# Attention and maxout MLP in one kernel: opening two products of the first layer when the first head group is done

## The chip, the cores and the metric

The kernel runs on one core of a Trainium2 chip. The metric is the device time of one execution in microseconds (us). Engines are named as in the profile: PE (TensorE), DVE (VectorE), ACT (ScalarE), POOL (GpSimd), SP (the queue that issues DMAs).

## The reference

For 8 batches of 8 heads, 576 positions and head size 64, two attentions are added: one over queries, keys and values that are averaged in fours (its output is repeated four times), and one in which each position sees only the positions less than 4 away. The sum, seen as 4608 tokens of 512 features, goes through a maxout MLP with 768 hidden features.

```python
out_d = sm_attn(q_d, k_d, v_d)            # pooled by 4
out_up = np.repeat(out_d, factor, axis=2)
mask = np.abs(pos[:, None] - pos[None, :]) < factor
scores = np.where(mask, scale * q @ k.T, -1e9)
x = out_up + softmax(scores) @ v          # -> (4608, 512)
h = np.maximum(np.maximum(x @ w1, x @ w2), x @ w3)
return h @ w_out
```

## The kernel before, in words

Nothing is issued where it is written. The program first records operations with their tiles; `place` (line 287) then plays a list scheduler with prices for each operation and gives every engine a fixed order, and `emit` (line 414, whence line 458 in all rows) issues in that order. An operation is offered when its inputs are done and its buffers can be had; among those offered an engine takes the one with the smallest priority number (`at(prio, lag)`, line 484), PE operations with a priority of 0 or more ahead of those with a negative one (line 210). The constants at lines 36 to 45 and 81 to 89 are lags, margins, priorities and prices of that scheduler. Buffers of one tag, PSUM banks too, are given out strictly in the order in which the tiles were written in the program (lines 312 to 328): a later tile of the tag cannot take a buffer before an earlier one has. There are four banks `pm`, three `pa` and one `pq` (line 481).

A head group n is four heads of one batch; a block j is the two groups 2j and 2j + 1 of a batch's first 512 positions. The first two blocks are computed on PE by `dense(j)` (line 1130): band scores (`band_scores`, two pairs of heads `pr`, each in two steps `tp` of two banks, softmax on DVE and ACT with maxima `mxb` and sums `zb`), pooled inputs (`band_sums`), band values (`band_values`, which transposes the probabilities in two banks for each pair and multiplies in `pq`), and the pooled attention (`pooled`, line 1136, through `tail_pooled`, `pooled_scores`, `band_pooled_values`, `pooled_values`). Block 0 uses the `pm` banks, block 1 the `pa` banks. The other blocks compute the band on DVE, POOL and ACT (`scores`, `values`).

`turn(j)` (line 1166) adds pooled and band outputs for each of four feature columns c (two from each head group) and splits the sum into a high and a low part, `xhi` and `xlo` (`transposes`, line 888). `mlp_column(j, ft, tag)` (line 910) computes one of six groups of 128 hidden features: for each of the three weights i it opens one bank and sums 12 products into it, for each column c high x high, low weight x high, high weight x low; then it takes the maximum. `mlp_out` (line 927) does the second layer. Weights arrive as 64-bit floats and are cut up in pieces by `weight_split` (line 570) on ACT and DVE: `weight_in(ft)` makes the three pieces of one hidden group, `whi` and `wlo`. Pieces have a priority of 39.08 plus 0.91 for each piece (line 1173).

The order in which block 0 is written (line 1152) gives the order of the `pm` banks: scores of group 0, values of group 0, scores of group 1, values of group 1, and only then, from `mlp_column(0, 0, "pm")` (line 1190), the first layer. The priorities of the groups are `FIRST` (line 43); `LATE` (line 44) is added for the loads of the pooled inputs (`late`, line 606): 37.8 for group 1.

Of the kernel before, what the change touches and what calls it, by code (L numbers as in the profile page):

```python
# [21 lines left out]
P = 128  # L22
# [5 lines left out]
NCC = DM // P  # L28
# [4 lines left out]
QS = 1.0 / 128.0  # L33
QB = 1.0 / 8.0
XBUFS = 5
LAG = 646.33
LAG0 = 272.7
MLP = 601.0
PE_LAG = 1784.3
BANK_LAG = 1458.35  # L40
SEG = FAC * P
NDENSE = 2
FIRST = (0.0, 5.15, 43.52, 45.57)
LATE = (0.0, 37.8, 0.0, 0.0)
WPRIO = (20.0, 60.0, 105.0, 150.0, 160.0, 170.0, 180.0)
SETS = (5, 4, 3, 2, 5, 4, 5, 5)
HOMES = ("whi5", "whi4", "whi3", "whi2", "pv", "pv", "whi5", "pv")
# [30 lines left out]

ENGINES = ("PE", "DVE", "ACT", "POOL", "SP")
DONE_NS = {"PE": 230.0, "DVE": 150.0, "ACT": 190.0, "POOL": 200.0}  # L80
SPARE = 1850.93
PATIENCE = {"PE": 0.0, "DVE": 294.88, "ACT": 136.05, "POOL": 0.0, "SP": 0.0}
LANES = 8
RING = 128
DMA_FIRST = 1300.0
# [1 line left out]
SLOW = 82000.0  # L87
SWITCH = {("R", "P"): 120.0, ("P", "R"): 110.0, ("P", "T"): 25.0, ("T", "P"): 93.0, ("t", "P"): 90.0, ("P", "t"): 90.0, ("B", "P"): 96.0, ("M", "P"): 100.0, ("P", "M"): 20.0, ("R", "T"): 10.0, ("T", "R"): 5.0, ("R", "M"): 91.0, ("T", "M"): 93.0, ("M", "R"): 300.0, ("M", "T"): 305.0, ("M", "B"): 0.0, ("B", "M"): 96.0, ("B", "R"): 120.0, ("t", "R"): 90.0, ("R", "t"): 95.0, ("t", "M"): 90.0, ("t", "B"): 90.0, ("t", "T"): 90.0, ("T", "t"): 90.0, ("M", "t"): 100.0}
COLD = 1.65


def is_ap(a):
# [56 lines left out]
class Recorder:  # L149
# [44 lines left out]
    def add(self, forms):  # L194

        o = Op()
        o.forms = forms
        outs, ins = [], []
        for method, args, kw in next(iter(forms.values())):
            named = [k for k in ("out", "accum_out") if is_ap(kw.get(k))]  # L200
            w = [kw[k] for k in named]
            r = [a for a in args if is_ap(a)] + [v for k, v in kw.items() if is_ap(v) and k not in named]
            if "out" not in named:
                w.append(args[0])
                r = r[1:]
            outs += w
            ins += r
        o.prio = self.prio
        if "PE" in forms and o.prio >= 0.0:
            o.prio -= 2000.0  # L210
        o.lag, o.spare, o.margin = self.lag, self.spare, 0.0
        if "PE" in forms and self.lag in (LAG, MLP):
            o.lag, o.margin = PE_LAG, BANK_LAG
        elif self.lag == MLP:
            o.lag = 0.0
        o.seq = len(self.ops)
        o.need, o.tiles = set(), []
        pe = "PE" in forms
        for write, aps in ((False, ins), (True, outs)):
            for ap in aps:  # L220
                r = self.region(ap)
                if r is None:
                    continue
                info, p0, p1, m = r
                bufs, order = self.tags[info["tag"]]
                assert info["k"] + bufs >= len(order), ("used after its buffer was given on", info["name"])
                for q, w, a0, a1, am, was_pe in info["acc"]:
                    if (w or write) and q is not o and (info["psum"] or (a0 < p1 and p0 < a1 and (am & m))):
                        o.need.add(q)
                if not info["ops"] or info["ops"][-1] is not o:  # L230
                    info["ops"].append(o)
                    o.tiles.append(info)
                if write and info["psum"] and pe:
                    info["acc"] = [x for x in info["acc"] if not (x[1] and x[5])]
                info["acc"].append((o, write, p0, p1, m, pe))
        self.ops.append(o)
        return o
# [49 lines left out]
    def place(self):  # L287
# [45 lines left out]
        while len(out) < len(ops):  # L333
# [30 lines left out]
            if e == "PE":  # L364
                kind = pe_kind(o)
                c += SWITCH.get((last_kind, kind), 0.0)
                last_kind = kind
            if e == "PE" and t < SLOW:
                c *= COLD
            o.eng, o.start = e, t  # L370
            if e == "SP":
# [98 lines left out]
def local_global_attention_maxout_kernel(ctx: ExitStack, tc: tile.TileContext, q, k, v, qt_dense, kt_dense, qt_pool, kt_pool, qkt_tail, v_dense, v_tail, w_in, w_out, ident_d, mask_d, band_d, out):  # L470
# [89 lines left out]
    def load_constants():  # L560
        for t in ptail + dtail:
            dve.memset(t, 0.0)
        load_band()
        for t in vt2:
            dve.memset(t[0:3, 0], 0.0)

# [340 lines left out]
        blk["lo"].append(lo)  # L907


    def mlp_column(j, ft, tag):  # L910
        blk = state["blk", j]
        t = new([P, 4 * P], tag="t", bufs=3, name=f"t_{j}_{ft}")
        for i in range(3):
            ps = bank([P, 4 * P], tag, f"ph_{j}_{ft}_{i}")
            ops = [(a[ft][:, i, c], b[c]) for c in range(NCC) for a, b in ((whi, blk["hi"]), (wlo, blk["hi"]), (whi, blk["lo"]))]
            for m, (a, b) in enumerate(ops):
                pe.matmul(ps, a, b, start=m == 0, stop=m == len(ops) - 1)
            if i == 0:
                act.copy(t, ps)
            else:  # L920
                dve.tensor_tensor(out=t if i == 1 else ps, in0=ps, in1=t, op=ALU.max)
        h = new([P, 2, 4 * P], F32R, tag=f"whi{ft}" if j == B else f"hh{ft}", name=f"h_{j}_{ft}")
        blk["h"][ft] = h
        act.copy(h[:, 0], ps)
        dve.tensor_tensor(out=h[:, 1], in0=ps, in1=h[:, 0].bitcast(F32), op=ALU.subtract)
# [204 lines left out]
    def dense(j):  # L1130
        tag = "pm" if j == 0 else "pa"
        ns = (2 * j, 2 * j + 1)
        state["blk", j] = {"x": [None] * NCC, "band": {}, "hi": [], "lo": []}
        prio = {n: FIRST[n] for n in ns}

        def pooled(n, _):
            tail_pooled(n)
            pooled_scores(n)
            band_pooled_values(n)
            pooled_values(n)  # L1140

        def step(n, f, *a):
            with at(prio[n], LAG0):
                f(n, *a)

        a, b = ns
        load = {n: [(n, band_load), (n, band_load_v)] for n in ns}
        scores = {n: [(n, band_scores, pr, tag) for pr in range(2)] for n in ns}
        sums = {n: [(n, band_sums, pr, tag) for pr in range(2)] for n in ns}
        values = {n: [(n, band_values, pr, tag) for pr in range(2)] for n in ns}  # L1150
        if j == 0:
            order = [load[a][0], load[b][0], load[a][1], load[b][1]] + scores[a] + sums[a] + values[a] + scores[b] + sums[b] + values[b] + [(a, pooled, 0), (b, pooled, 0)]
        else:
            order = load[a] + scores[a] + sums[a] + values[a] + load[b]
            order += [scores[b][0], sums[b][0], (a, pooled, 0), values[b][0], scores[b][1], sums[b][1], values[b][1], (b, pooled, 0)]
        for x in order:
            step(*x)
# [5 lines left out]
                attention(n)  # L1163
        rec.spare = 0.0

    def turn(j):
        with at(-200.0, LAG0 if j < 2 else LAG):
            for c in range(NCC):
                transposes(j, c)

    def weights(f, *which):
        for x in which:
            with at(39.08 + state["pieces"] * 0.91):
                f(x)

    with at(-2.0):
        load_constants()
    dense(0)
    weights(weight_in, 0, 1, 2)
    turn(0)  # L1180
    weights(weight_in, 3)
    weights(weight_out, 0, 1, 2, 3)
    dense(1)
# [63 lines left out]
```

## Time and profile before

| | us |
|---|---|
| median of 3 runs | 742.31 (741.31 to 744.15) |
| profiled execution, its own time | 743.23 |
| span of the profiled execution | 741.5 |
| PE busy in the span | 716.1 (97%) |
| DVE busy | 643.0 (87%) |
| ACT busy | 438.8 (59%) |
| POOL busy | 364.2 (49%) |

The profiled execution is 0.92 us above the median; 1.73 us of its time lie around the span. Busy shares are means over stages with different limits, so the stage matters: the queries below cut the span. Every row carries line 458, since one helper issues everything, so rows are told apart by their tiles: `xhi_0r`, `xlo_0r`, `whi_0r`, `wlo_0r` are the split activations and weights of the first layer, `hqk` the weight piece being cut up, `whi`, `wlo` without `_0r` buffers that hold the band's inputs and probabilities early on, `nm` and `pa` belong to the pooled attention.

### The profile page before, as it was taken

Reading aid. Unit: us, or ns where it says so; the run is one execution under the profiler, and the core shown is the slowest. Engines: PE = TensorE matmul, PEld = TensorE weight load, DVE = VectorE, ACT = ScalarE, POOL = GpSimd, SP = SyncE. Lnnn points to the kernel's source line nnn. Section 1 sums busy time; section 2 is a strip of 40 time slices with the busy share of each in tenths; the row PEclk is TensorE's granted clock in tenths of the full one; section 3 lists DMA queues with packets and bytes.
Section 4 is the critical chain, followed back from the end, with each engine's and each line's share of the span. In section 5 each row is a group of like instructions: output and inputs, shape, how many; then the busy total and the mean of one; then the engine's idle time right before and its main releaser. Section 6 shows DMA issues by size and latency. Waiting matters only on the chain.

```text
span 741.5 us, 11907 instructions
## 1 busy us (share of the span) xinstructions
PE 716.1 (97%) x3820; PEld 569.4 (77%) x3820; DVE 643.0 (87%) x961; ACT 438.8 (59%) x1486; POOL 364.2 (49%) x563
## 2 busy tenths in 40 slices
PE   5977999999999999999999999999999999999996
PEld 3765677878787877778877887788778888888885
DVE  6999998999989996989989997979998999988520
ACT  4776867627595738657484849575785646433221
POOL 0100001139895977668387949495875735321000
PEclk9969899999999999999999999999999999999999
DMA  8943334365645362555346434532442310000012
GB/s 285 360 168 124 101 91 143 96 201 180 193 127 181 122 194 83 153 165 178 93 130 190 150 103 150 166 98 87 153 122 89 107 60 15 2 1 0 1 57 57
DMA packets 51561, 92.21 MB, mean 124 GB/s; under 512 B 5644, under 2 KB 21310, under 8 KB 51498
## 3 DMA queue, kind: packets, MB, share of 16 engines
q1 hardware_dynamic: 51498, 91.45, 39.2%
q8 instruction: 30, 0.49, 0.3%
q14 instruction: 33, 0.27, 0.1%
HBM read 81.99 MB, written 9.44 MB: 123 GB/s over the span
## 4 chain that ended last, share of the span: by engine, by line
PE 89%; DVE 4%; ACT 2%; DMA 2%; POOL 1%; issue 0%; SPq 0%; ACTq 0%; POOLq 0%; DVEq 0%
PE pm L458 73%; PE pa L458 14%; PE pq L458 2%; DVE hqk L458 1%; ACT wlo L458 1%; DVE x L458 1%; DMA hh<-in_w_in_dram 1%; DMA v<-in_v_dram 1%; DMA whi<-in_kt_dense_dram 1%; DVE wlo_0r L458 1%; DVE mxb L458 0%; POOL pv L458 0%; DVE xlo_0r L458 0%; DVE t L458 0%; SPq L458 0%
## 5 line engine op out<-in xcount | busy, mean ns | idle before, releaser
L458 PE MATMUL pm<-xhi_0r,whi_0r 128*128 128x512 f32 x552 | 219.2, 397 | 0.8 <-ACT xhi_0r L458 0.8
L458 PE MATMUL pm<-xhi_0r,wlo_0r 128*128 128x512 f32 x552 | 218.7, 396 | 0.0
L458 PE MATMUL pm<-xlo_0r,whi_0r 128*128 128x512 f32 x552 | 218.5, 397 | 0.0
L458 ACT ACTIVATE pv<-v,sums 128x64 f32<-128x64 f32 x604 | 158.1, 416 | 12.6 <-POOL sums L458 9.1
L458 POOL TENSOR_TENSOR pv<-v,sums 128x256 f32<-128x256 f32 x227 | 137.6, 708 | 5.9 <-DMA v<-in_v_dram 5.2
L458 PE MATMUL pm<-wo_0r,hh_0r 128*128 128x512 f32 x576 | 137.4, 393 | 0.0
L458 PEld LDWEIGHTS pm<-wo_0r,hh_0r 128*128 128x128 f32 x576 | 107.0, 188 | 23.4 <-issue 0.9
L458 PEld LDWEIGHTS pm<-xhi_0r,whi_0r 128*128 128x128 f32 x552 | 104.4, 189 | 23.5 <-issue 1.1
L458 PEld LDWEIGHTS pm<-xlo_0r,whi_0r 128*128 128x128 f32 x552 | 104.5, 189 | 22.3 <-issue 0.8
L458 PEld LDWEIGHTS pm<-xhi_0r,wlo_0r 128*128 128x128 f32 x552 | 104.6, 189 | 22.0 <-issue 0.9
L458 DVE TENSOR_REDUCE sums<-prod 128x28 f32<-128x1792 f32 x56 | 113.5, 2027 | 0.4
L458 DVE TENSOR_TENSOR prod<-k,pq 128x1792 f32<-128x1792 f32 x56 | 112.4, 2007 | 0.5
L458 DVE TENSOR_REDUCE x<-pv 128x256 f32<-128x1792 f32 x34 | 73.5, 2162 | 10.2 <-ACT pv L458 8.2
L458 POOL TENSOR_TENSOR pv<-pv 128x768 f32<-128x768 f32 (+1 forms) x44 | 68.3, 1552 | 6.0 <-ACT pv L458 4.2
L458 ACT CAST hh_0r<-pm 128x512 fp32r<-128x512 f32 x48 | 28.4, 591 | 48.8 <-DVE pm L458 48.6
L458 ACT COPY y<-pm 128x512 f32<-128x512 f32 x46 | 26.8, 589 | 48.9 <-PE pm L458 43.7
L458 POOL TENSOR_TENSOR hv<-v 128x128 f32<-128x128 f32 (+1 forms) x49 | 23.7, 488 | 37.5 <-DVE vd L458 25.4
L458 DVE TENSOR_TENSOR t<-pm,t 128x512 f32<-128x512 f32 x46 | 35.4, 770 | 6.6 <-PE pm L458 4.7
L458 ACT COPY t<-pm 128x512 f32<-128x512 f32 x44 | 26.1, 593 | 23.1 <-PE pm L458 22.9
L458 DVE TENSOR_TENSOR hh_0r<-pm,hh_0r 128x512 fp32r<-128x512 f32 x48 | 32.8, 684 | 6.2 <-ACT hh_0r L458 5.8
L458 DVE TENSOR_TENSOR pm<-pm,t 128x512 f32<-128x512 f32 x46 | 31.9, 693 | 5.6 <-PE pm L458 5.0
L458 ACT ACTIVATE pa<-pa,nm 128x144 f32<-128x144 f32 x80 | 28.4, 355 | 12.9 <-DVE sums L458 4.3
(322 smaller groups left out, 1104.9 us busy)
## 6 DMA issues: line engine op xcount, KB each, us to landing
k<-in_k_dram SPq DMA_DIRECT2D x55, 320.0 KB
v<-in_v_dram SPq DMA_DIRECT2D x54, 320.0 KB
out_dram<-y SPq DMA_DIRECT2D x36, 256.0 KB
q<-in_q_dram SPq DMA_DIRECT2D x56, 128.0 KB
hqk<-in_qt_pool_dram SPq DMA_DIRECT2D x24, 256.0 KB
hqk<-in_kt_pool_dram SPq DMA_DIRECT2D x24, 256.0 KB
hh<-in_w_in_dram SPq DMA_DIRECT2D x10, 512.0 KB
pv<-in_w_in_dram SPq DMA_DIRECT2D x5, 512.0 KB
```

The lines of the kernel that those rows point to most:

```text
L458: getattr(self.engines[o.eng], method)(*map(real, args), **{k: real(x) for k, x in kw.items()})
```

## The change

Block 0's order is written anew: the pooled attention of group 0 and a new step, `first_half`, come ahead of the values of group 1. `first_half` writes down the pieces of the first hidden group's weights, turns the first two feature columns, and opens `PRE` = 2 banks `pm` (for two of the three weights of hidden group 0), into each of which it sums the 6 products of these two columns. The banks stay open, marked `held`; `mlp_column(0, 0)` later adds the 6 products of the other two columns to each. The third bank is computed whole, as before. The remaining columns are turned later. One element is copied on ACT among the constants. Priorities, lags and margins of the scheduler change, and it prices PE at the low clock only from 11 us on (`WARM`). The number of products is the same.

```diff
-LAG = 646.33
-LAG0 = 272.7
+LAG = 634.25
+LAG0 = 241.08
-PE_LAG = 1784.3
-BANK_LAG = 1458.35
+PE_LAG = 1474.1
+BANK_LAG = 1235.52
-FIRST = (0.0, 5.15, 43.52, 45.57)
-LATE = (0.0, 37.8, 0.0, 0.0)
+FIRST = (0.0, 6.25, 45.82, 47.05)
+LATE = (1.3, 0.0, 6.8, 9.5)
-SPARE = 1850.93
-PATIENCE = {"PE": 0.0, "DVE": 294.88, "ACT": 136.05, "POOL": 0.0, "SP": 0.0}
+SPARE = 2066.22
+PRE = 2
+PATIENCE = {"PE": 0.0, "DVE": 313.5, "ACT": 117.54, "POOL": 0.0, "SP": 0.0}
+WARM = 11000.0
-            if e == "PE" and t < SLOW:
+            if e == "PE" and WARM < t < SLOW:
                 c *= COLD
         load_band()
+        act.copy(dtail[1][:1, :1], dtail[0][:1, :1])
+    def part(ps, j, ft, i, chunks):
+        blk = state["blk", j]
+        ops = [(c, a[ft][:, i, c], b[c]) for c in chunks for a, b in ((whi, blk["hi"]), (wlo, blk["hi"]), (whi, blk["lo"]))]
+        for m, (c, a, b) in enumerate(ops):
+            pe.matmul(ps, a, b, start=c == 0 and m == 0, stop=c == NCC - 1 and m == len(ops) - 1)
+
+    def first_half(n, _):
+        weights(weight_in, 0)
+        turn(0, (0, 1))
+        with at(-100.0):
+            for i in range(PRE):
+                state["pre", i] = bank([P, 4 * P], "pm", f"ph_0_0_{i}")
+                rec.of[state["pre", i].tensor.name]["held"] = True
+                part(state["pre", i], 0, 0, i, (0, 1))
     def mlp_column(j, ft, tag):
         for i in range(3):
-            ps = bank([P, 4 * P], tag, f"ph_{j}_{ft}_{i}")
-            ...
+            if j == ft == 0 and i < PRE:
+                ps = state["pre", i]
+                part(ps, j, ft, i, (2, 3))
+            else:
+                ps = bank([P, 4 * P], tag, f"ph_{j}_{ft}_{i}")
+                part(ps, j, ft, i, range(NCC))
-            order = [load[a][0], load[b][0], load[a][1], load[b][1]] + scores[a] + sums[a] + values[a] + scores[b] + sums[b] + values[b] + [(a, pooled, 0), (b, pooled, 0)]
+            order = [load[a][0], load[b][0], load[a][1], load[b][1]] + scores[a] + sums[a] + values[a] + scores[b] + sums[b] + [(a, pooled, 0), (a, first_half, 0)] + values[b] + [(b, pooled, 0)]
-    def turn(j):
+    def turn(j, chunks=range(NCC)):
-            for c in range(NCC):
+            for c in chunks:
                 transposes(j, c)
-            with at(39.08 + state["pieces"] * 0.91):
+            with at(40.46 + state["pieces"] * 1.24):
                 f(x)
-    weights(weight_in, 0, 1, 2)
-    turn(0)
+    weights(weight_in, 1, 2)
+    turn(0, (2, 3))
```

## Rows read from the trace of the kernel before

**Rows 1.** The page of the profile, busy time: of each engine the busy time in us, its share of the span, and the number of instructions.

```profile
PE 716.1 (97%) x3820; PEld 569.4 (77%) x3820; DVE 643.0 (87%) x961; ACT 438.8 (59%) x1486; POOL 364.2 (49%) x563
```

**Rows 2.** Busy time by stretch. Columns: the stretch in us from the span's start, its length, then per engine the busy time with the number of instructions in brackets, then the granted clock as a share of 2.4 GHz, the busy share of the DMA engines, and GB/s.

```profile
39.00:41.00 2.00, 0.03 (x4) 0.00 (x0) 1.90 (x8) 1.28 (x4) 0.00 (x0) 1.00 1.06 364
41.00:43.17 2.17, 0.58 (x9) 0.41 (x9) 2.14 (x8) 1.45 (x7) 0.00 (x0) 0.59 0.50 177
43.17:51.30 8.13, 7.55 (x56) 6.32 (x56) 7.50 (x21) 6.98 (x30) 0.00 (x0) 0.50 0.23 81
51.30:62.00 10.70, 9.10 (x78) 6.17 (x76) 10.41 (x26) 8.28 (x22) 1.43 (x2) 0.82 0.62 195
62.00:76.35 14.35, 11.15 (x56) 7.70 (x56) 14.14 (x38) 8.93 (x32) 0.37 (x1) 0.86 0.25 77
76.35:738.00 661.65, 657.81 (x3396) 527.11 (x3395) 575.39 (x763) 388.83 (x1307) 359.61 (x551) 1.00 0.36 112
```

**Rows 3.** The chain of work that ended last, in order of time, asked for 50 to 80 us: start, duration, what was on the chain.

```profile
53.35 0.69 DVE wlo_0r L458
...
75.48 0.83 ACT wlo L458 x4
...
76.35 2.62 PE pa L458 x13
```

**Rows 4.** The timeline of PE: start, duration, engine, line, operation, out<-in, shapes, count, and in square brackets the idle time ahead of it and what ended it. `pm`, `pa` and `pq` are PSUM banks.

```profile
41.50 0.58 PE L458 MATMUL pq<-ident,wlo 32*6 32x32 f32 x8 [2.47 <-DVE wlo L458]
43.17 1.97 PE L458 MATMUL pm<-ident,wlo 128*128 128x128 f32 x8 [1.09 <-ACT wlo L458]
45.71 2.30 PE L458 MATMUL pq<-y,wo 128*64 128x128 f32 x16 [0.57 <-ACT wlo L458]
...
51.31 0.79 PE L458 MATMUL pm<-xhi_0r,whi_0r 128*128 128x512 f32 x1
...
61.96 0.80 PE L458 MATMUL pm<-xhi_0r,whi_0r 128*128 128x512 f32 x1 [0.76 <-ACT xhi_0r L458]
```

**Rows 5.** The timeline of ACT, same columns. An ACTIVATE from `pm` with `mxb` is one exponential of the band softmax.

```profile
8.60 1.28 ACT L458 ACT_TABLE_LOAD   x1 [8.60 <-DVE mxb L458]
9.90 0.37 ACT L458 ACTIVATE wlo<-pm,mxb 128x134 f32<-128x134 f32 x1
...
37.02 1.19 ACT L458 CAST xhi_0r<-t 128x512 fp32r<-128x512 f32 x2
...
42.30 0.37 ACT L458 ACTIVATE wlo<-pm,mxb 128x134 f32<-128x134 f32 x1 [0.72 <-DVE mxb L458]
...
45.05 0.38 ACT L458 ACTIVATE wlo<-pm,mxb 128x134 f32<-128x134 f32 x1
...
55.57 0.59 ACT L458 COPY x<-pq 128x512 f32<-128x512 f32 x1 [0.82 <-PE pq L458]
```

**Rows 6.** The timeline of DVE, same columns. `wlo_0r<-hqk,whi_0r` writes the low half of one weight piece; the low halves of pieces 1 and 2 (counted from 0) are shown.

```profile
11.61 0.42 DVE L458 TENSOR_TENSOR hv<-v 128x256 f32<-128x256 f32 x1 [1.43 <-DMA v<-in_v_dram]
...
12.54 0.43 DVE L458 TENSOR_TENSOR hv<-v 128x256 f32<-128x256 f32 x1 [0.37 <-DMA v<-in_v_dram]
12.88 0.17 DVE L458 TENSOR_SCALAR zb<-zb 128x8 f32<-128x8 f32 x1
...
37.71 1.30 DVE L458 TENSOR_TENSOR xlo_0r<-t,xhi_0r 128x512 fp32r<-128x512 f32 x2 [0.27 <-ACT xhi_0r L458]
...
39.00 0.69 DVE L458 TENSOR_TENSOR wlo_0r<-hqk,whi_0r 128x512 fp32r<-128x512 f32 x1
...
52.41 0.68 DVE L458 TENSOR_TENSOR wlo_0r<-hqk,whi_0r 128x512 fp32r<-128x512 f32 x1
...
60.32 1.54 DVE L458 TENSOR_TENSOR t<-x,od 128x512 f32<-128x512 f32 x2
```

**Rows 7.** The timeline of PE again, two places: products at the low clock, and a run of 41 products at the full clock, of which the first and the last are shown.

```profile
62.55 1.05 PE L458 MATMUL pm<-xhi_0r,wlo_0r 128*128 128x512 f32 x2
63.41 1.05 PE L458 MATMUL pm<-xlo_0r,whi_0r 128*128 128x512 f32 x2
64.26 0.63 PE L458 MATMUL pm<-xhi_0r,whi_0r 128*128 128x512 f32 x1
...
284.46 0.48 PE L458 MATMUL pm<-xhi_0r,whi_0r 128*128 128x512 f32 x1
...
293.66 0.39 PE L458 MATMUL pm<-xhi_0r,wlo_0r 128*128 128x512 f32 x1
```

**Rows 8.** Busy time by stretch, columns as in group 2, for the stretches in which the granted clock is low.

```profile
41.00:42.00 1.00, 0.50 (x8) 0.40 (x8) 1.00 (x3) 0.58 (x2) 0.00 (x0) 0.69 0.82 288
42.00:55.00 13.00, 11.34 (x81) 8.94 (x81) 12.17 (x37) 11.14 (x41) 0.00 (x0) 0.50 0.31 104
62.00:65.00 3.00, 3.00 (x7) 2.38 (x8) 2.96 (x9) 0.80 (x3) 0.37 (x1) 0.50 0.14 56
76.00:82.00 6.00, 5.65 (x23) 4.02 (x22) 5.80 (x15) 5.02 (x19) 0.00 (x0) 0.50 0.28 100
```

**Rows 9.** The timeline of SP's DMA issues: start, how long the issue held the queue, and what is loaded.

```profile
12.54 3.78 SPq L458 DMA_DIRECT2D hh<-in_w_in_dram  x6
16.43 0.36 SPq L458 DMA_DIRECT2D traw<-in_qkt_tail_dram  x1
...
18.25 2.63 SPq L458 DMA_DIRECT2D v<-in_v_dram  x2
```

More of the change, by code (lines that the diff above doesn't have):

```diff
@@ L225, in add @@
                 bufs, order = self.tags[info["tag"]]
-                assert info["k"] + bufs >= len(order), ("used after its buffer was given on", info["name"])
+                assert info.get("held") or info["k"] + bufs >= len(order), ("used after its buffer was given on", info["name"])
                 for q, w, a0, a1, am, was_pe in info["acc"]:
@@ L913, in mlp_column @@
         for i in range(3):
-            ps = bank([P, 4 * P], tag, f"ph_{j}_{ft}_{i}")
-            ops = [(a[ft][:, i, c], b[c]) for c in range(NCC) for a, b in ((whi, blk["hi"]), (wlo, blk["hi"]), (whi, blk["lo"]))]
-            for m, (a, b) in enumerate(ops):
-                pe.matmul(ps, a, b, start=m == 0, stop=m == len(ops) - 1)
+            if j == ft == 0 and i < PRE:
[4 more added lines that the diff above has]
+                part(ps, j, ft, i, range(NCC))
             if i == 0:
```

## The prediction, made before the changed kernel ran

> **What bounds it now.** I read the page's busy line first: PE is busy 97% of the span, the next engine 87% [rows 1]. A mean over the span hides where the other 3% is, so I cut the span by stage next [rows 2]. From 76.35 us to 738 us PE is busy 657.81 of 661.65 us at the full clock: there, nothing but the amount of matmul work left sets the end. Between 39 and 76.35 us PE stands idle for 1.97 + 1.59 + 0.58 + 1.60 + 3.20 = 8.94 us, and its granted clock is low. The reader is to see that the kernel has two regimes: a start in which PE waits, and a long full stretch whose length is fixed by what was left over. The chain that ended last says the same: without a gap on VectorE from 53.35 us, by way of ScalarE at 75.48 us, to PE at 76.35 us, and on PE from there [rows 3]. So a product of the first layer that PE does in a hole ahead of 76.35 us comes off the end; one moved inside the full stretch is worth nothing.
>
> The PE timeline shows the holes: 2.47 us ahead of 41.50, 1.09 ahead of 43.17, 0.57 ahead of 45.71, and the first product of the layer only at 51.31, after the second group's transposes into the `pm` banks [rows 4]. Its operands are there earlier: xhi of the first two columns is cast from 37.02 [rows 5], xlo ends at 39.01 (37.71 + 1.30), the low half of the second weight piece at 39.69 (39.00 + 0.69) [rows 6]. So the first layer could have begun at about 39 us, and what forbids it is the order in which the four `pm` banks are handed out. That order is what the change edits.
>
> **The change, part by part.**
>
> Twelve products (two banks, two columns, three products each) move from 51 us and later to the hole from 39 to 51.3 us. That hole is 1.97 + 1.59 + 0.58 = 4.14 us [rows 2]. A product costs 0.43 us at the low clock (two from 62.55, two from 63.41, the next at 64.26) and 0.230 us at the full one (40 steps from 284.46 to 293.66 take 9.20 us) [rows 7]. Twelve therefore need 2.76 us at the full clock and 5.2 us at the low one. Where they leave, PE can go on with later products: the third piece is cut up by 53.09 (52.41 + 0.68), the fourth by 54.04 (53.35 + 0.69), and from 62 us the other two columns are there [rows 3, 4, 6]. Counted at the end, where a product is 0.230 us, the gain is **2.76 us**. The bounds: nothing, if the banks come too late, and 4.14 us, the whole hole.
>
> The clock. It is 1.2 GHz (0.50) from 42 to 55 us, from 62 to 65 and from 76 to 82 [rows 8], each time after a stretch with holes: 0.03 us of work between 39 and 41 [rows 2], 0.76 us idle ahead of 61.96 [rows 4]. With the first hole filled I expect the first fall to be put off. Of the 11.34 us of PE work in it, half would be saved, but until the third piece is cut up at 53.09 PE has no other product to put in its place, so only the rest to 55 us counts: half of 1.7 us or a little more, **0.85 us**. The other two falls I leave; if they went too, half of 3.00 and of 5.65 us [rows 8] would be 4.3 us more. So 0 to 5.2 us.
>
> A one-element copy on ScalarE is put at the start, so that the function table is loaded there: 1.28 us at 8.60, with the first exponential at 9.90, go off that chain [rows 5]. VectorE does not gain it all: it waits for v to land, starts the second hv at 12.54 and takes up zb at 12.88 only then [rows 6]. I take **0.3 us** between 0 and 1.28. The page "ScalarE: Activation LUTs" of the Trainium skill (What ACT_TABLE_LOAD costs) adds a drain of about 1.38 us to a load of 1.283 us, which would make the upper end here 2.66 us; no drain stands in the trace, where the exponential follows the load at once, so the measurement decides.
>
> The open banks. Two of the four `pm` banks are taken from the second group's transposes until the column is finished. Before, these take the first banks that the second group's exponentials give back, at 43.17; now they need the next two, whose exponentials end at 45.43 (45.05 + 0.38) [rows 4, 5]: up to 2.3 us later. Nobody waits for that yet: the copy that ends the group is done at 56.16 (55.57 + 0.59) and its user, the sum into t, comes at 60.32 [rows 5, 6], 4.2 us of cover. I cost it at nothing; without the cover it is 2.3 us.
>
> The DMA queue. The second group's pooled loads lose their added priority of 37.8 and go ahead of the six weight pieces. Those six are issued at 12.54 to 16.32; the pooled loads now hold the queue from 16.43 to 20.88 (18.25 + 2.63) [rows 9]. So the weight pieces can come up to 4.45 us later and the second group's pooled part earlier by about as much. Piece two is wanted at 39 us, VectorE is busy 1.90 of 2.00 us just then [rows 2], so I take 0; the loss is priced under the rivals, and a gain of up to 1.5 us is possible, since the last two columns (61.96, with its 0.76 us wait [rows 4]) hang on that pooled part.
>
> The new lags, margins and priorities reorder the rest. After 76.35 us there is 3.84 us of idle time in all [rows 2], which includes the end of the kernel, so little can be won; how much a worse order could lose no row tells. I take 0, with half of that idle time, 1.9 us, either way.
>
> Sum: 2.76 + 0.85 + 0.3 = 3.9 us off the profiled execution of 743.23 us (span 741.5 and 1.73 around it): 739.3. That execution lies 0.92 us above the median of 742.31, so against the median **738.4 us**. A measurement of this kernel can tell about 0.5%, 3.7 us, from no change, so the line is at 738.6 and the forecast sits on it.
>
> **The rivals.**
>
> *The clock stays up.* If the filled hole also keeps the second and third falls from coming, 5.2 us instead of 0.85 count: 2.76 + 5.2 + 0.3 = 8.2, so 734.1 us. For it: each fall stands right behind a hole [rows 2, 8]. Against it: of the holes between 62 and 76.35 us, 3.20 us in all [rows 2], most belong to the second pair of groups, whose work the change moves only by its priorities. The Trainium skill, "TensorE: Matmul & The Clock Gate" (The HAM clock gate), says that the throttled clock is the default and activity releases it; the trace agrees at 41 us, where the clock falls to 0.69 and then 0.50 after two almost empty microseconds.
>
> *It does not do what it says.* All four `pm` banks hold the second group's scores until the exponentials that begin at 42.30 [rows 5]. If these do not come earlier, no bank can be opened before about 43.1, and the hole of 1.97 + 1.59 us is over. Then only 0.58 us and the table load's 0.3 are won: 741.5 us, no change. For it: xhi, xlo and these exponentials are ordered behind each other on VectorE. Against it: the planner now has work to put there, and the second group's pooled part is freed from its delay.
>
> *Slower: the second open bank holds up the second group.* Banks are given out in the written order, so the transposes cannot take a bank until both new ones are open, and the second opens with a product that needs weight piece two. It decides from the point at which that piece is more than 43.17 - 39.69 = 3.5 us later than now; the loads moved ahead of it allow 4.45 us [rows 4, 6, 9]. Then PE stands empty about 0.97 us more, up to 5.2 us of cold products go ahead of the transposes, 6.1 us in all against a cover of 4.2, and 1.9 us reach the VectorE chain: 742.31 + 0.97 + 1.9 = 745.2 us, more with any further fall of the clock. Against it: VectorE has idle time ahead of 13 us, and the piece's 39.69 is set by VectorE's order more than by its landing.
>
> **How the numbers follow.** Forecast 0.42 (own range 736.5 to 740.3, half of it under 738.6), clock 0.22, does not do it 0.20, slower 0.16 (three quarters of it over 746.0 once a further fall is counted). Faster by over 0.5%: 0.21 + 0.22, and a little for the second pair's pooled part, 0.45. Slower: 0.12. Within: 0.43. The range runs from 732.5 (the clock's case with more of the table load and of the hole) to 744.0, which leaves out most of the slower case.
>
> **What would show it.** Right: the table load in the first 3 us; xhi products on PE ahead of 46 us, twelve ahead of the second group's last transposes; PE idle between 39 and 51.3 us under 2 us; a granted clock above 0.50 there; the last hole still near 76 us, and PE full behind it. Wrong: the first such product only after 46 us (banks); a PE wait just ahead of it on a weight piece, with the transposes behind it (slower case); or the last hole moved past 80 us, by which all gain ahead of it would be lost.

## The result, and the profile after

The changed kernel takes 747.89 us (median of 7 runs, 745.20 to 749.83); the kernel before, run beside it, 742.01 us. The ratio is 1.0070 (95% interval 1.0053 to 1.0088): slower by 0.7%, where 738.4 us was forecast with a range up to 744.0. Two more sets of runs of the unaltered changed kernel gave 1.0049 (1.0018 to 1.0079) and 1.0063 (1.0038 to 1.0088), so the cost is 3.6 to 5.2 us by the three ratios, 2.9 to 5.9 us by the medians.

The page's busy line after, which answers to [rows 1]:

```profile
span 746.1 us, 11901 instructions
PE 715.0 (96%) x3820; PEld 567.0 (76%) x3820; DVE 640.2 (86%) x961; ACT 438.0 (59%) x1477; POOL 376.1 (50%) x571
```

PE is busy 1.1 us less than before in a span that is 4.6 us longer: it waits more. The stretches of [rows 2] after (columns as there):

```profile
39.00:41.00 2.00, 0.09 (x2) 0.00 (x0) 1.97 (x10) 1.30 (x4) 0.00 (x0) 0.91 0.42 149
41.00:43.17 2.17, 1.75 (x11) 1.38 (x12) 2.17 (x9) 2.04 (x11) 0.00 (x0) 0.50 0.46 139
43.17:51.30 8.13, 7.46 (x58) 5.99 (x57) 6.85 (x21) 7.77 (x30) 0.00 (x0) 0.74 0.56 170
51.30:62.00 10.70, 7.78 (x82) 5.12 (x82) 10.56 (x22) 7.17 (x18) 0.00 (x0) 1.00 0.50 161
62.00:76.35 14.35, 9.23 (x53) 6.27 (x51) 14.18 (x37) 8.29 (x27) 2.42 (x3) 1.00 0.21 65
76.35:738.00 661.65, 657.15 (x3382) 525.24 (x3382) 571.91 (x760) 387.79 (x1302) 371.81 (x561) 0.99 0.36 112
```

The hole from 39 to 51.3 us shrank from 4.14 to 3.00 us, and behind 43.17 us the clock in it rose (0.74 for 0.50); from 51.3 us the work is done at the full clock with more idle time in between, so PE is further on at 76.35 us although it idled longer. That much is the forecast, as far as a count of products goes (more on that below the table). Now the stretch behind 76.35 us, cut finer, first before:

```profile
76.35:85.00 8.65, 8.65 (x58) 6.30 (x58) 8.45 (x19) 7.66 (x24) 0.00 (x0) 0.65 0.30 96
85.00:95.00 10.00, 10.00 (x89) 7.43 (x90) 8.79 (x21) 7.85 (x25) 0.00 (x0) 1.00 0.42 129
140.00:160.00 20.00, 20.00 (x89) 16.33 (x88) 19.56 (x25) 7.77 (x15) 4.94 (x8) 1.00 0.45 130
```

and after:

```profile
76.35:85.00 8.65, 8.38 (x59) 5.57 (x58) 8.38 (x20) 7.25 (x26) 0.00 (x0) 0.80 0.39 124
85.00:95.00 10.00, 7.93 (x80) 6.06 (x76) 6.20 (x14) 5.67 (x16) 0.00 (x0) 0.84 0.20 58
140.00:160.00 20.00, 19.01 (x93) 14.64 (x92) 19.76 (x29) 8.76 (x20) 3.66 (x5) 1.00 0.26 71
```

Before, PE has no idle time at all here. After, it stands 2.07 us between 85 and 95 us and 0.99 us between 140 and 160, and VectorE does 2.6 us less between 85 and 95. PE's timeline after, which answers to [rows 4], names the waits:

```profile
42.00 0.79 PE L460 MATMUL pm<-xhi_0r,whi_0r 128*128 128x512 f32 x1 [0.41 <-ACT wlo L460]
45.15 1.91 PE L460 MATMUL pm<-ident,wlo 128*128 128x128 f32 x8
90.40 1.09 PE L460 MATMUL pq<-y,wo 128*64 128x128 f32 x16 [2.07 <-ACT wlo L460]
140.91 0.49 PE L460 MATMUL pm<-xhi_0r,whi_0r 128*128 128x512 f32 x1 [0.26 <-ACT whi_0r L460]
143.13 0.50 PE L460 MATMUL pm<-xhi_0r,wlo_0r 128*128 128x512 f32 x1 [0.51 <-DVE wlo_0r L460]
149.12 0.39 PE L460 MATMUL pm<-xlo_0r,whi_0r 128*128 128x512 f32 x1
```

The first product stands at 42.00 us (51.31 before), seven of them ahead of the second group's transposes at 45.15. The last row is the last of the 216 products of block 0's first layer; before it begins at 145.15. Behind ScalarE at 90 us stands a load, on ScalarE and VectorE:

```profile
89.44 0.66 ACT L460 ACTIVATE hqk<-hh 128x512 f32<-128x512 f32 x1 [2.38 <-DMA hh<-in_moe_w_out_dram]
90.13 0.43 DVE L460 TENSOR_SCALAR hqk<-hqk 128x512 f32<-128x512 f32 x1 [3.57 <-ACT hqk L460]
```

This is the absolute value with which the cutting of an output-weight piece begins; the copy that PE waits for is queued behind it on ScalarE (90.00 us), the second pair's maxima behind its cut on VectorE. In the kernel before the same copy stands ahead of the waiting absolute value:

```profile
87.53 0.36 ACT L458 COPY wlo<-pq 6x256 f32<-6x256 f32 x1
88.38 0.68 ACT L458 ACTIVATE hqk<-hh 128x512 f32<-128x512 f32 x1 [0.49 <-DVE wlo_0r L458]
```

The loads in question are issued on SP closer together than before. After, then before:

```profile
78.75 0.33 SPq L460 DMA_DIRECT2D pv<-in_w_in_dram  x1
81.94 2.12 SPq L460 DMA_DIRECT2D hh<-in_moe_w_out_dram  x2
```

```profile
82.74 0.33 SPq L458 DMA_DIRECT2D hh<-in_moe_w_out_dram  x1
87.03 0.33 SPq L458 DMA_DIRECT2D hh<-in_moe_w_out_dram  x1
```

The second of two begins at 83.72 after (81.94 + 2.12 less its own 0.33), 1.8 us behind the first; before, 4.3 us lie between them. That alone does not make a load late: before, the load issued at 82.74 lands at 87.77 us, 5.0 us after its issue and nearly as late as the 5.6 us of the one issued at 83.72 after (most others of this size need 3.3 to 3.6 us in this part of both profiles). A late load stands in both kernels; what differs is what the new order has queued behind it.

A measure that runs through all profiles is the count of block 0's first-layer products (216) that PE has begun by a time:

| profile | by 51.3 | by 85 | by 95 | by 120 | last begins | span |
|---|---|---|---|---|---|---|
| before | 0 | 45 | 62 | 133 | 145.15 | 741.5 |
| after | 10 | 55 | 64 | 128 | 149.12 | 746.1 |
| after, second profile | 10 | 55 | 69 | 140 | 146.31 | 742.8 |
| after, third profile | 10 | 55 | 64 | 133 | 147.86 | 744.5 |
| constants alone | 0 | 42 | 59 | 129 | 147.02 | 744.1 |
| copy alone | 3 | 45 | 64 | 137 | 144.40 | 740.7 |
| opening undone | 0 | 51 | 60 | 127 | 149.93 | 749.1 |
| short loads | 10 | 55 | 69 | 140 | 146.41 | 743.4 |
| load elsewhere | 10 | 55 | 67 | 138 | 146.81 | 743.0 |
| ready products ahead | 10 | 55 | 65 | 135 | 148.71 | 747.1 |
| load elsewhere and ready products ahead | 10 | 55 | 72 | 143 | 147.04 | 744.8 |
| cheap cuts, after | 10 | 55 | 62 | 117 | 151.61 | 749.0 |
| cheap cuts, before | 3 | 47 | 68 | 145 | 142.50 | 738.6 |

From the last product to the end it is 596.1 to 597.4 us in all of these but "opening undone" (599.2) and the two with ready products of the second layer put ahead (598.4 and 597.8). So most of the span's difference is there at that product: ten products ahead at 85 us, behind at 145. Between the two orders the count at an earlier time is no measure of the lead, since the new order has other work of PE elsewhere: with the opening undone it is still 6 ahead of the kernel before at 85 us, 51 against 45. Only profiles of one order can be compared by it.

### The profile page after: what moved, and what is told of

The parts are those of the page before. It is cut to its first block, busy times and chain, and to the rows that moved or that the text cites. A ratio compares the mean times of both kernels' runs of the same rounds, so it can differ in the third digit from the quotient of the medians.

```text
span 746.1 us, 11901 instructions
## 1 busy us (share of the span) xinstructions
PE 715.0 (96%) x3820; PEld 567.0 (76%) x3820; DVE 640.2 (86%) x961; ACT 438.0 (59%) x1477; POOL 376.1 (50%) x571
## 5 line engine op out<-in xcount | busy, mean ns | idle before, releaser
L460 DVE TENSOR_TENSOR prod<-k,pq 128x1792 f32<-128x1792 f32 x56 | 114.8, 2049 | 1.5 <-ACT pq L460 0.5
L460 POOL TENSOR_TENSOR pv<-pv 128x768 f32<-128x768 f32 (+1 forms) x52 | 80.6, 1551 | 7.3 <-ACT pv L460 5.2
L460 DVE TENSOR_REDUCE x<-pv 128x256 f32<-128x1792 f32 x30 | 60.6, 2020 | 11.2 <-ACT pv L460 7.2
L460 DVE TENSOR_TENSOR t<-pm,t 128x512 f32<-128x512 f32 x46 | 33.1, 720 | 12.6 <-PE pm L460 10.7
L460 POOL TENSOR_TENSOR vs<-th 128x64 f32<-128x64 f32 x13 | 4.3, 328 | 73.3 <-PE pa L460 73.2
L460 ACT COPY pq<-q 128x256 f32<-128x256 f32 x56 | 22.0, 393 | 28.7 <-DVE prod L460 27.6
```

The lines of the kernel that those rows point to most:

```text
L460: getattr(self.engines[o.eng], method)(*map(real, args), **{k: real(x) for k, x in kw.items()})
```

## The experiments

**The change again, twice.** Unaltered.

> The changed kernel once more, for a second profile. Theory A (the opening puts PE ahead by about 9 products, 2 us, until 85 us, and a late landing of a weight load at 87 to 89 us, which holds up ACT, DVE and PE in turn, takes the lead away): the wait of ACT for that load and the PE hole of about 2 us near 88 us are there again, time near 747 to 748. Rival B (the hole was an accident of the one profiled execution): no PE hole over 1 us between 84 and 92 us, and the time is still near 747 to 748, so that the loss lies elsewhere. In both, PE idle between 51.3 and 76.35 us is near 8 us against 4.8 before.

Measured: 746.16 us (744.61 to 753.17), ratio 1.0049 (1.0018 to 1.0079).

> The changed kernel once more, unaltered, on the same chip as the three runs beside it: 745 to 748 us, with its last product of block 0's first layer at 146 to 149.5 us. What differs between its own profiles (146.31 and 149.12) is, by the theory, how late the two output-weight loads land at 88 to 90 us; by the rival, chance that is spread over the whole span.

Measured: 746.26 us (745.07 to 751.47), ratio 1.0063 (1.0038 to 1.0088). PE's hole ahead of the same instruction is 1.26 and 1.47 us instead of 2.07; both have the waits at 138 to 142 us as the first profile does (0.25 and 0.50, 0.27 and 0.50). The losses belong to the kernel, the size of the first varies with the execution. PE's idle time between 51.3 and 76.35 us, expected near 8 us again, is 5.52 and 6.66 us after 8.04.

**The change in parts.** Structure alone (the new order of writing, `first_half`, `part`, `PRE`; every constant as before, no copy), constants alone (with `WARM`, no opening, no copy), the copy alone:

```diff
+        act.copy(dtail[1][:1, :1], dtail[0][:1, :1])
```

> Only the opening of the two products, the split turn and the new order of block 0; every priority, lag, margin and price as before, and no copy at the start. Theory A and theory N (the new numbers are to blame, not the opening): 738 to 742 us, first product of the first layer before 46 us. Rival S (the opening itself costs: two banks fewer for the second group, more holes behind): 745 us or more.

> Only the new priorities, lags, margins and the price at the low clock from 11 us on; the first layer opens as before, and no copy at the start. Theory N (the new numbers are to blame): 745 us or more. Rival S (the opening costs): 740 to 743 us. If both this and the opening alone are slow, the two do not add up and the order as a whole decides.

> Only the one-element copy on ACT at the start. The table load moves to the first 3 us and the first exponential to about 8.6 us. By the prediction's term 0.3 us are gained (741.7); by its upper end 1.28 us (740.7). A theory by which any disturbance of an order costs time (the kernel before stands on a lucky order) gives 743 or more.

Measured: structure alone 758.48 us, ratio 1.0207 (1.0165 to 1.0250); constants alone 745.27, 1.0026 (1.0007 to 1.0045); copy alone 743.21, 1.0010 (0.9987 to 1.0032). The copy is worth nothing that can be measured. The constants alone cost 2 us: the order is dealt anew, and two of the last four weight pieces come 0.1 and 0.7 us after their first product instead of well ahead. The structure under the old constants has the same kind of hole:

```profile
91.43 1.09 PE L460 MATMUL pq<-y,wo 128*64 128x128 f32 x16 [2.20 <-ACT wlo L460]
```

and loses some 12 us more behind the layer, where PE waits 4.1 us for ScalarE's `pd` among others. The new constants go with the new structure, then; they buy back most of this, not all.

**The opening alone undone.** The ten early products (operations 292 to 301) are taken out of the planned order and put back ahead of operation 359, behind the second group's transposes; nothing else moves:

```diff
+    first = [o for o in out if 292 <= o.seq <= 301]
+    rest = [o for o in out if not 292 <= o.seq <= 301]
+    k = next(x for x, o in enumerate(rest) if o.seq == 359)
+    out = rest[:k] + first + rest[k:]
```

> The changed kernel with every other instruction in its place, but TensorE's ten products of the two opened banks are done behind the second group's transposes, at about 51 us, as in the kernel before, instead of from 42 us: the opening alone is undone. Theory (the last weight pieces, not the amount of matmul work, set the end of block 0's first layer in the changed kernel): the 10 products are missing at 51.3 us (0 to 3 instead of 10) and some 8 of them are still missing at 76.35 us, but the last product of that layer starts at 146 to 149 us as in the changed kernel (146.31 and 149.12 in its two profiles), and the time lies within 1 us of the changed kernel's. Rival (the opening gives its 2 to 2.8 us and the rest of the change costs some 6): the time rises by 2 to 3 us above the changed kernel's, to 748 to 750.

Measured: 748.33 us (747.60 to 750.89), ratio 1.0081 (1.0064 to 1.0098), against 746.26 and 1.0063 for the changed kernel beside it. The medians are 2.07 us apart, the ratios 0.0018 (1.3 us), and the intervals of the ratios overlap, so the times alone do not tell the two apart. The profiles do, for the start. Ahead of one instruction PE waits 2.0 us for VectorE in each profile of the changed kernel; here it is with the opening, and with it undone:

```profile
75.90 0.28 PE L460 MATMUL pq<-ident,wlo 32*6 32x32 f32 x4 [2.00 <-DVE wlo L460]
```

```profile
78.32 0.28 PE L491 MATMUL pq<-ident,wlo 32*6 32x32 f32 x4 [2.01 <-DVE wlo L491]
```

The other two profiles of the changed kernel have it at 75.36 and 75.78 us, and the seven runs below that alter nothing ahead of 76 us at 75.14 to 77.11. So the opening brings this place forward, by 2.4 to 3.0 us against the unaltered kernel and by 1.2 us at the least. Behind it the hole at 90 us, which varies with the execution, blurs the difference: the last product begins at 149.93 us, against 146.31 to 149.12. The count misled me here too: I expected some eight products to be missing at 76.35 us, and 45 of 46 had begun. My theory that the pieces make the lead worthless is not borne out: the last piece came 2.1 us later than in the third profile as well, with the same distance to its first product. The rival was nearer: **the opening gives 1.2 to 3.2 us at 76 us, and 1.3 to 2.1 us in the time, where it is not clear of noise; the rest of the change costs some 5 to 8 us** (an estimate: what the opening gives, on top of the 3.6 to 5.2 us by which the changed kernel is slower).

**The late loads.** The output-weight loads shortened in the changed order, to the first 256 of the 1024 words of each partition; the rest of those weights is left out:

```diff
-        sp.dma_start(flat, src)
+        load = sp.dma_start(flat, src)
+        if len(view) == 3:
+            load.cut = 256
```

> The changed kernel with every instruction in its place, but each of block 0's output-weight loads (four for the first feed-forward, two later) moves only the first 256 of the 1024 words of each partition, so it lands earlier; the rest of those weight pieces is left out of the load and so holds whatever was there. Theory (the loads land late in the changed kernel, the absolute value on ScalarE stands behind them, VectorE's cuts behind that, and the last input-weight pieces come 3 to 6 us later than before): between 76 and 165 us ScalarE's wait for these loads (5.2 us) and VectorE's wait for ScalarE's absolute value (6.6 us) shrink to 2 us or less together, the low halves of pieces 16 and 17 (143.08 and 146.67 us in the profile of the changed kernel) come at 141 us or earlier, the last product of block 0's first layer starts at 143 to 146 us instead of 149.12, and the time falls by 2 to 5 us to 742 to 745. Rival (the later part of the re-dealt order, not the landing, costs the time): the waits go but the time stays within 1 us of the changed kernel's 746 to 748.

Measured: 745.11 us (742.81 to 749.04), ratio 1.0024 (1.0007 to 1.0042): 1.8 to 3.4 us less than the changed kernel's three ratios. ScalarE's timeline at the load, and two stretches as above:

```profile
88.16 0.67 ACT L461 ACTIVATE hqk<-hh 128x512 f32<-128x512 f32 x1 [0.25 <-DMA hh<-in_moe_w_out_dram]
```

```profile
85.00:95.00 10.00, 10.00 (x112) 7.83 (x109) 8.36 (x18) 6.16 (x17) 0.00 (x0) 1.00 0.09 28
140.00:160.00 20.00, 19.52 (x84) 15.80 (x85) 19.67 (x26) 8.31 (x18) 3.71 (x5) 1.00 0.27 82
```

The hole at 90 us is gone and VectorE has more of its work back (8.36 of 10.00 us, for 6.20). That the short loads take time off is seen in the ratios, though their interval overlaps two of the three. That they do it by this hole is argued and not shown: the second profile of the unaltered kernel has a hole of 1.26 us there and the same counts (69 by 95 us, 140 by 120) with its last product at 146.31, and in the profile with short loads PE stands 1.25 us ahead of 82.12 us instead. The second loss, behind 138 us, is as in the changed kernel: the waits of 0.25 and 0.50 us, and the last product at 146.41.

Three ways to the same end that leave no work out. Another place for the third load that shares the DMA engines (`put_off` moves one instruction back in the planned order as far as data and buffers allow; 927 is that load); the waiting absolute values and cuts put back; a plan with 2600 ns of lag between such a load and its absolute value:

```diff
+    put_off(out, 927, 9000.0)
```

> The changed kernel, with one DMA issue moved: the load of the first weight piece of the fifth hidden group, issued at 78.75 us and first read at 107.70, goes behind the two output-weight loads that are issued at 81.94 and 83.72 us and waited for at 88 to 89. Theory (three loads of 512 KB within 5 us share the DMA engines, where the order counts on each alone): ScalarE's wait for the output weights at 88 to 89 us (1.58 to 2.38) goes below 1 us, TensorE's hole behind it (1.26 to 2.07) below 0.7 us, and the time falls by 1 to 2 us against the changed kernel, to 744.3 to 745.3. Rival (the wait is the loads' own issue, which hangs on VectorE): no change.

```diff
+    for seq in (517, 516, 515, 514, 513, 525, 524, 523, 522, 521):
+        put_off(out, seq, 2500.0)
```

> The changed kernel, with only the absolute values and cuts of block 0's first two output-weight pieces put 2.5 us further back in ScalarE's and VectorE's own orders, so that the copy TensorE waits for at 89 to 90 us and the second pair's maxima go ahead of them. Theory (the two loads, issued 1.8 us apart, land later than the order counts on, and what TensorE needs stands behind them on ScalarE): TensorE's idle 1.26 to 2.07 us ahead of 89 to 90 us go below 0.5 us, the lead over the kernel before at 95 us is 5 products or more as in the quicker of the two profiles, and the time falls by 1 to 2 us, to 744.5 to 746. Rival (the lead is lost again at 140 us, where the last pieces come): the hole goes, the time stays within 0.5 us.

```diff
-        act.activation(a, high.bitcast(F32), AF.Abs)
+        with at(rec.prio, lag):
+            act.activation(a, high.bitcast(F32), AF.Abs)
```

> The changed kernel, with the order dealt anew after one number: the absolute value of each of block 0's output-weight pieces is counted as due 2.6 us later behind its load, so that ScalarE is given other work before it. Theory (ScalarE stands behind a late landing): its wait for these loads and VectorE's wait behind it fall below 3 us together, the last product of block 0's first layer starts at 143 to 147 us, and the time falls to 741 to 745, where the opening shows as a gain or no change against before. Rival (any new deal of the order costs or gives a few us by its own, as the constants alone did with 745.27): the waits fall and the time is 745 to 749 all the same.

Measured: 746.92 us, 1.0050 (1.0030 to 1.0070); 750.14, 1.0091 (1.0067 to 1.0115); 756.29, 1.0179 (1.0148 to 1.0209). The load elsewhere leaves a wait of 1.40 us and a hole of 1.08 in its profile, just under what the changed kernel has. It says little of whether three loads share the DMA engines: the third is issued at 84.27 us now, 0.42 us behind the one that is waited for (83.85), and is in flight together with it. The cuts put off do away with the hole at 90 us and make one further on:

```profile
100.84 1.27 PE L489 MATMUL pa<-qkT 64*128 64x144 f32 x4 [2.27 <-ACT wlo L489]
```

The new plan moved the whole stretch and its last product began at 157.67 us. Each of these orders has a late instruction of its own.

**The last pieces.** First the cutting made cheap, in both kernels' orders: the cuts of the pieces behind the sixteenth work on 16 columns of each row, and the rest is left out:

```diff
+        if state["pieces"] > 16:
+            for o in rec.ops[seq + 1 : seq + 5]:
+                o.cut = 16
```

> The changed kernel with every instruction in its place, but for block 0's last eight weight pieces (two of the six feature blocks of the first layer and two of the output weights, after the sixteenth piece) the four cutting operations behind the absolute value work on 16 columns of each row of 128 or so instead of all; the rest of those pieces is left out. Theory (TensorE catches up with the pieces, so that the time at which the last ones are cut sets the end of the first layer): the last pieces come several us earlier, the last product of block 0's first layer starts at 143 to 146 us instead of 149.12, and the time falls by 3 us or more, to 744 or less; the 9 products of lead that the opening gave at 76.35 us are then seen in the time. Rival (what is lost after 76 us is not lost to the pieces): the time falls by less than 1 us.

> The same cut of work in the kernel before: four cutting operations of block 0's last eight weight pieces on 16 columns of a row, the rest left out. Theory: in the kernel before, the last piece is ready 2.5 us or more ahead of its first product, TensorE does not wait for pieces, and the time stays within 1 us of before (741 to 743). Rival (VectorE's and GpSimd's load in this stretch holds up TensorE in other ways as well, the same in both kernels): the time falls by as much as the changed kernel's does under the same cut.

Measured: 747.85 us, 1.0077 (1.0045 to 1.0109), and 742.91, 0.9997 (0.9980 to 1.0014). The kernel before does not care, as the theory had it. The time of the changed one does not fall either, though VectorE is busy only 11.14 of 20 us from 120 to 140 us then. In its profile PE no longer waits for the last pieces: their low halves end 0.8 us ahead of use instead of 0.05, and the stretch from the 121st product of the layer to the last takes 30.77 us instead of 31.82 to 31.84 in the changed kernel's three profiles. So the waits for the last pieces are worth about 1 us, not the 3 that I had expected; this profile (750.78 us, 2.9 above its median) had lost more than that by 120 us, where it has 117 products. The pieces come but 1 us nearer to their products with most of the cutting gone, which points at their place in line. Then the line itself: the second layer's ready products ahead of the late pieces on PE; this with the load moved; and the cuts 4 us earlier on VectorE and ScalarE, with the first two output-weight pieces put off as above:

```diff
+    first = [o for o in out if 1225 <= o.seq <= 1236]
+    for o in first:
+        advance(out, o.seq, o.start - 138200.0)
```

> The changed kernel, with TensorE's order altered at one place: the second layer's first twelve products, ready by 136 us, go ahead of the last two pieces of the first layer, where TensorE stands before pieces that are not cut up yet. Theory: the waits for these pieces at 138 to 146 us (0.72 to 0.99 us of idle time, and 2.1 us of work lost to the kernel before between 120 and 160 us) shrink to 0.3 us, and the time falls by 1 to 2 us, to 744.3 to 745.3. Rival (the pieces move back with TensorE, since their cuts stand behind attention's steps): the time stays within 0.5 us.

> Both edits together. Theory: the two add up, 2 to 4 us below the changed kernel, 742.3 to 744.3, level with the kernel before: what is then left against the opening's 1.6 to 2 us is the 1 us that the new constants lose behind 160 us. Rival: less than the better of the two alone.

```diff
+    for seq in range(943, 975):
+        advance(out, seq, 4000.0)
```

> As the run with the cuts put off, and beside it every operation of block 0's last four input-weight pieces stands up to 4 us earlier in the orders of VectorE and ScalarE, as far as buffers and data allow; TensorE's order is untouched. Theory: the low halves of the last two pieces come 1.5 to 3 us ahead of where the changed kernel has them against their first products (margins from -2.2 and -0.9 us to 0 or more), the last product of block 0's first layer starts at 142.5 to 145 us, ahead of the 145.15 of the kernel before, and the time is 740 to 743: the opening's lead is seen in the time at last. Rival (attention's steps, now later on VectorE, hold up TensorE by as much): margins improve, but the last product starts at 146 us or later and the time is 744 to 747.

Measured: 749.84 us, 1.0083 (1.0064 to 1.0102); 749.63, 1.0093 (1.0075 to 1.0112); 759.59, 1.0222 (1.0206 to 1.0239). None of my theories here holds. With PE's gap filled, the wait of 0.5 us for the late low half is gone, and PE waits for the next weight piece instead; with the cuts early, for the softmax behind them. The run with both has no hole at 90 us and the most products of the changed orders by 120 us (143), and its last product still begins only at 147.04. PE's waits in the runs e14 and e11:

```profile
154.90 1.46 PE L490 MATMUL pm<-wo_0r,hh_0r 128*128 128x512 f32 x4 [2.17 <-ACT wo_0r L490]
```

```profile
136.12 1.97 PE L491 MATMUL pa<-ident,wlo 128*128 128x128 f32 x8 [4.74 <-DVE wlo L491]
```

From 140 to 160 us VectorE is full before and after alike (19.56 and 19.76 of 20 us), and it serves two customers of PE there, weights and attention. In the orders tried here, whichever was put first, the other was late; the order of the kernel before, in which PE has no idle time there, shows that it need not be so. No version with the new structure or the new constants is as fast as the kernel before; the nearest are the short loads, which leave work out, and the constants alone.

## Why the prediction was wrong

**The failing step** is "there, nothing but the amount of matmul work left sets the end", said of 76.35 to 738 us. It holds for the order of the kernel before: three profiles with that order (before, the copy, the cheap cuts) begin the last product at 145.15, 144.40 and 142.50 us, and their spans are 741.5, 740.7 and 738.6, so a lead at the last product arrives whole, and one at the first product (51.31, 49.82 and 47.83) for the most part. I took this for a property of the stage. It is one of the order, and the change deals a new one. A PE that is busy 10.00 of 10.00 us shows no slack and no lack of it; how close its inputs run has to be read on the side that delivers. In the kernel before the last piece's low half ends on GpSimd at 140.15 us (138.85 + 1.30), 2.7 us ahead of the first product that reads it:

```profile
138.85 1.30 POOL L458 TENSOR_TENSOR wlo_0r<-hqk,whi_0r 128x512 fp32r<-128x512 f32 x1
142.88 0.39 PE L458 MATMUL pm<-xhi_0r,wlo_0r 128*128 128x512 f32 x1
```

After, the same half begins on VectorE at 145.99 and ends at 146.67, 0.05 us ahead of that product:

```profile
145.99 0.68 DVE L460 TENSOR_TENSOR wlo_0r<-hqk,whi_0r 128x512 fp32r<-128x512 f32 x1
146.72 0.50 PE L460 MATMUL pm<-xhi_0r,wlo_0r 128*128 128x512 f32 x1
```

For the piece ahead of it the margin went from 7.0 to 0.06 us, with PE waiting 0.51 us (143.13, above).

The prediction had a sign for this: "the last hole moved past 80 us, by which all gain ahead of it would be lost". That sign came, with the hole at 88 to 90 us; but no rival put a mechanism or a price to it.

Point by point:
- **The opening** (2.76 us): right at the start. The first product stands at 42.00 us, so the rival in which no bank can be had before about 43.1 did not occur. Ten of the twelve products were ahead of 51.3 us, and undoing them puts the same instruction, at 76 us, 2.4 to 3.0 us later than in the three profiles of the changed kernel. How much of it reaches the end is 1.3 us by the ratios and 2.1 by the medians, and not clear of noise.
- **The clock** (0.85 us, or 5.2 in the rival): the profile after has the rival's clock, 1.00 from 51.3 to 76.35 us, and the time is worse all the same. Its other profiles have 0.86 and 0.93 there, the kernel before and its near copies 0.84, 0.91 and 0.87, so in this stretch executions of one kernel differ by as much as the change could give. The full clock gave PE's work sooner and more idle time behind it; in the profile after the hole at 90 us cost clock too (0.84 from 85 to 95 us).
- **The table load** (0.3 us): it moved to the start as forecast,

```profile
0.73 1.28 ACT L460 ACT_TABLE_LOAD   x1 [0.73 <-PEq L1251]
2.02 0.19 ACT L460 COPY dtail<-dtail 1x1 f32<-1x1 f32 x1
8.59 0.37 ACT L460 ACTIVATE wlo<-pm,mxb 128x134 f32<-128x134 f32 x1 [6.37 <-DVE mxb L460]
```

  and the first exponential comes 1.3 us earlier, but the copy alone changes the time by 0.10% (-0.13 to 0.32%), nothing that can be told.
- **The open banks** (0): the transposes came 2.0 us later (45.15 for 43.17), inside the 2.3 allowed, and the cover held: the copy that ends the group is done at 55.91 us, and its user comes at 59.89. The slower rival's number, 745.2, lies close to the result, but its mechanism did not occur: no weight piece held the transposes up.
- **The DMA queue** (0): right for the first pieces; the second was cut by 34.42 us, earlier than the 39.69 of before. The loads that mattered were others, 45 us further on, which I had not looked at.
- **Lags and order** (0, 1.9 either way): the mis-sized term. I bounded it by half the idle time behind 76.35 us, as if a new order could only shift what idle time there was. In place of 0 it measured some 5 to 8 us of loss, worked out as 3.6 to 5.2 us slower plus the 1.2 to 3.2 us that the opening gives. Of it 1.8 to 3.4 us went with the short loads, by the ratios; that this is the hole at 85 to 95 us is argued. The waits of 0.75 to 0.77 us for the last piece but one went with the cheap cuts, and with them 1.05 us of that stretch in one profile. The constants alone cost 2 us without a hole at 90 us. Which constant does it, and how the rest divides, stays open.

Two sums of the rivals are a tenth off and decide nothing: 2.76 + 5.2 + 0.3 is 8.3, and 742.31 less 0.88 is 741.4.

## What to carry to other kernels

When an edit makes a scheduler deal a new order, the order is part of the edit's cost, and a fully busy engine in the old profile is no bound on it: read how far ahead of use each input arrives. A small margin is a warning, not a bound (2.7 us here, and some 5 to 8 were lost). Look also at what stands in an engine's queue behind an instruction that waits for a late load: a late load cost PE no idle time in the old order, and 1.3 to 2.1 us in three profiles of the new one. Undoing one part inside the new order (here ten instructions moved back) separates the idea from the re-dealing at the price of one run; compare the same instruction in both profiles, since the times may not tell them apart, and a count of products does not compare across orders.

## What the runs showed of the hardware

- A load is done when its last piece is. Of the 512 KB load issued at 83.72 us, 15 of 16 landings are in by 87.61 us and the last at 89.36. ScalarE starts at 89.44. The Trainium skill says the same ("DMA: Bandwidth & Descriptors", Why a DMA increments its semaphore by 16 and not by 1): the engines finish independently and only the full count means that all data landed. A 16 KB packet of instructions was moved from 85.81 to 87.24 us. Such a packet and a last landing 0.8 to 1.8 us behind the fifteenth go together at this place in the kernel before, in all three profiles of the changed one and with the opening undone; with the load elsewhere the packet is there, and the last landing comes 0.06 us behind the fifteenth. The traces do not name the DMA engine of a packet, so that the packet is the cause is not shown.
- With the same order, the first product of the layer begins at 51.31, 49.82 and 47.83 us (before, the copy, the cheap cuts before): 3.5 us of spread, of which 2.9 are left in the span.
- The runs of the changed kernel spread further (744.61 to 753.17 in one set) than those of the kernel before beside them (740.97 to 747.45); the hole at 90 us, which hangs on when a load lands, was 1.26 to 2.07 us in three profiles, and 0.47 us in the run with ready products put ahead, which alters nothing in front of 138 us.
